# Linear attention and a two-layer expert on one core: the keys' maxima sent through DRAM, the large px matmuls split over quarters of the array, and the first large block's attention begun earlier

## The chip, the cores and the metric

One core of a Trainium2 chip runs the whole program. The metric is device microseconds of one execution; lower is better. The kernel before takes 844.15 us (median of three runs, 844.1 to 846.15). The execution that was profiled took 839.7 us, of which the page's span is 837.9.

## The reference

```python
def _attn_ref(q, k, v):                      # (8, 8, 576, 64) each
    q_s = np.exp(q - np.max(q, axis=-1, keepdims=True))
    q_s = q_s / (np.sum(q_s, axis=-1, keepdims=True) + 1e-09)
    k_s = np.exp(k - np.max(k, axis=2, keepdims=True))
    k_s = k_s / (np.sum(k_s, axis=2, keepdims=True) + 1e-09)
    kv = np.einsum('bhsd,bhse->bhde', k_s, v)
    return np.einsum('bhsd,bhde->bhse', q_s, kv).astype(np.float32)

def _moe_ref(x, w_in, w_out):                # x (4608, 512), w_in (512, 2048), w_out (2048, 512)
    h = x @ w_in
    relu6 = np.clip(h + 3.0, 0.0, 6.0)
    g = h * relu6 / 6.0
    return (g @ w_out).astype(np.float32)
```

The attention's output, heads side by side, is x. The softmax of the keys runs over the 576 tokens of a batch, so every key channel has one maximum for each batch; the queries' runs over the 64 channels of a head. The weights come as float64.

## The kernel before

**Tokens.** The 4608 tokens are taken as three small blocks of 512 and three large blocks of 1024. A batch has 576 tokens, so a block straddles batches. Heads go in four pairs (hp): two heads of 64 channels fill 128 partitions.

**Small blocks (0, 1, 2).** For each of 16 chunks of d_ff, gemm1 makes `ph` (12 matmuls of 128x512), relu6 and a split into a high and a low part make `gp` on ACT and DVE, and gemm2 adds into four `po` banks (12 matmuls), one chunk later. A product in float32 is made of three fp32r matmuls: high x high, high x low, low x high.

**Large blocks (0, 1, 2).** They use seven products of half-size blocks for each pair of chunks instead of eight. Phase 1 makes h from the "factors" of x (`factors`, tiles `right`: seven high and low splits of blocks of x and of differences of them) and from sums of weights; phase 2 multiplies by w_out likewise. These weights are made during small blocks 1 and 2 (`sum_weights`, `plain_weights`), kept in DRAM (`wf`) and fetched again, two of 56 slots to a transfer, into `gp` and `left` tiles.

**Attention.** `token_attention` makes x for one block and one head pair. It is a generator; each yield is a point at which the main loop goes on with matmuls of the expert. Its steps are: loads of the queries and, for a batch whose kv is not yet there, of the keys twice (`kt`, channels on partitions, and `ke`, tokens on partitions) and the values; DVE's maximum over `kt` into `km` (L355), one number for each channel, copied over 128 columns by POOL into `kb` (L357), and the queries' softmax and transposition (`q_softmax_t`, DVE with help of ACT and POOL); PE turns `kb` round into the bank `pm` (L363), so that each partition has the maxima of all channels in a row, DVE subtracts it from `ke` (L364), ACT takes exp; an empty step; `kv_of`: ten float32 matmuls of 128x64 for a batch, two heads in two halves of the columns, into the bank `pkv`, and a kv tile of 128x128 in which the two heads' 64x64 blocks lie on the diagonal and the rest is zero; last px: for each 512 tokens, a float32 matmul of that kv tile with the transposed queries for every batch that they touch, copied by ACT into x (L385; in small blocks split into high and low).

`pm`, `pkv` and `px` share two PSUM banks (pool `ps_a`). A float32 matmul shows as two records, two passes, in the trace. 24 pairs of batch and head pair go through `token_attention`; batches 0 and 1 go through the older `attention`.

**What sets the order.** A scheduling layer records the instructions and orders each engine's queue. From block 1 on PE's order is that of the program (`in_order`). `steps` strings the units of a block together (L734): a unit's px comes after the next unit's loads. In blocks 1 and 2 each chunk calls it twice; in the large blocks every second slot calls it. Block 1 carries the attention of block 2, block 2 that of large block 0, and large block s that of s + 1. Block 2's last two chunks call `factors` three times each, and the rest of it, under a high priority, follows the block. `behind` puts instructions behind the ones listed in `front`, which are those of phase 2's last split (L590).

**Buffers.** `kt` has one buffer, `km` and `kb` two, `v` three, `gp` four. All loads and stores but four are issued by SP, whose queue is in order: an issue that waits holds up those behind it. `sum_weights` takes two `v` tiles (w4 and sums) and writes its parts to `gp` tiles. `store` takes `v` tiles.

Of the kernel before, what the change touches and what calls it, by code (L numbers as in the profile page):

```python
# [1 line left out]

# [16 lines left out]
P = 128  # L19
# [13 lines left out]
def attention_moe(  # L33
# [82 lines left out]
    FROM_DRAM = 3  # L116
    whole = dr.tile([P, NFC, 2 * DM], F32, name="whole")

    def split(hi, lo, src):
        return nc.scalar.copy(hi, src), nc.vector.tensor_sub(lo, src, hi.bitcast(F32))  # L120

    front = []

    def behind(units, count=1):

        with ExitStack() as order:
            for ins in front:
# [129 lines left out]
    def attention(j, hp):  # L257

        if not j:
            kt, qt, qT, vt, ke = first[hp]  # L260
        else:
            kt, ke, vt = load_k(j, hp)
# [25 lines left out]

    def load_k(b, hp, tokens=False):
        kt = att.tile([P, S], F32, name="kt", bufs=1)  # L290
        nc.sync.dma_start(kt, kT[b, hp])
        ke = att.tile([P, NCH, P], F32, name="ke", bufs=2)
        if tokens:
            nc.sync.dma_start(ke, k[b, hp].rearrange("p c h d -> p c (h d)"))
        vt = att.tile([P, NCH, 2, D + 1], F32, name="vt", bufs=2)
        nc.sync.dma_start(vt, v[b, hp])
        return kt, ke, vt

# [16 lines left out]
    def q_softmax_t(qt):  # L315
# [13 lines left out]
        qT = moe.tile([P, 2 * DM], F32, name="m", bufs=1)[:, 0:n]  # L329
        nc.vector.transpose(qT, qt)  # L330
        return qT

# [8 lines left out]
    def token_attention(t0, n, hp, put):  # L341

        need = [b for b in range(t0 // S, (t0 + n - 1) // S + 1)]
        qt = att.tile([P, SB], F32, name="qt", bufs=1)[:, 0:n]
        at = (t0 - TURNED) // TB
        nc.sync.dma_start(
            qt.rearrange("p (b n) -> p b n", n=TB),
            qf[at : at + n // TB, hp].rearrange("b p n -> p b n"),
        )
        loads = {b: load_k(b, hp, tokens=True) for b in need if (b, hp) not in kvs}  # L350
        yield
        new = {}
        for b, (kt, ke, vt) in loads.items():
            km = att.tile([P, 1], F32, name="km", bufs=2)
            nc.vector.tensor_reduce(km, kt, axis=AX.X, op=ALU.max)  # L355
            kb = att.tile([P, P], F32, name="kb", bufs=2)
            nc.gpsimd.tensor_copy(kb, km.broadcast_to([P, P]))  # L357
            new[b] = ke, vt, kb
        qT = q_softmax_t(qt)
        yield  # L360
        for ke, vt, kb in new.values():
            pm = bank_a("pm")
            flip(pm[:, 0:P], kb)  # L363
            nc.vector.tensor_sub(  # L364
                ke, ke, pm[:, 0:P].rearrange("p (o n) -> p o n", o=1).broadcast_to([P, NCH, P])
            )
            nc.scalar.activation(ke, ke, AF.Exp)
        yield
        yield
        for b, (ke, vt, kb) in new.items():  # L370
            kv_of(b, hp, ke, vt)
        yield
        for c in range(n // TB):
            px = bank_a("px")
            at = t0 + c * TB
            for b in need:
                lo, hi = max(b * S - at, 0), min((b + 1) * S - at, TB)
                if lo < hi:
                    mm(px[:, lo:hi], kvs[b, hp], qT[:, c * TB + lo : c * TB + hi], True, True)
            put(c, hp, px)  # L380
        yield

    def sb_attention(s):
        def put(c, hp, px):
            nc.scalar.copy(x_of(s)[:, hp, c * TB : (c + 1) * TB], px)  # L385

        return [token_attention(START + s * SB, SB, hp, put) for hp in (0, 2, 1, 3)]

    def block_attention(j):
        def put(c, hp, px):  # L390
            x_hi, x_lo = x_block(j)
# [19 lines left out]

    def keep(pair, side, block, src):
        nc.sync.dma_start(kept[side][:, SLOT[side][pair, PRODUCT[block]]], src)

# [11 lines left out]
    def sum_weights(pair, side):  # L426
# [17 lines left out]
        nc.vector.tensor_sub(s4, a12, s2)  # L444
        for i in range(2):
            dst = moe.tile([P, 2, TB], F32R, name="gp", bufs=4).rearrange("p i n -> p (i n)")
            four = dst.rearrange("p (k e n) -> p k e n", k=2, e=2)
            src = sums[:, i * TB : (i + 1) * TB].rearrange("p (k n) -> p k n", k=2)
            split(four[:, :, 0], four[:, :, 1], src)
            for k_ in range(2):  # L450
                block = (S1, S2, S3, S4)[2 * i + k_]
                keep(pair, side, block, dst[:, k_ * TB : (k_ + 1) * TB].bitcast(F32))
        yield
# [69 lines left out]
    def relu6(g, r, h):  # L523
        nc.scalar.activation(r, h, AF.Relu, bias=three, scale=1.0)  # L524
        nc.vector.scalar_tensor_tensor(g, r, 6.0, h, op0=ALU.min, op1=ALU.mult)  # L525

    def phase1(s):
        xb, yb, zb = {}, {}, {}
        for i, (p, n) in enumerate(SLOTS1):
# [24 lines left out]
            with tc.high_priority():  # L554
                if n == 1:
                    nc.scalar.copy(h11, x)
                if n == 0:
                    nc.vector.tensor_add(h11, h11, z)  # L558
                    relu6(h11, temp(), h11)
                if n == 3:  # L560
                    nc.scalar.copy(h21, x)
                if n == 2:
                    nc.scalar.copy(h22, y)
                if n == 4:
                    nc.vector.tensor_add(h22, h22, x)  # L565
                if n == 5:
                    relu6(h12, temp(), x)
                if n == 6:
                    nc.vector.tensor_add(h21, h21, y)  # L569
                    r = moe.tile([P, 2 * DM], F32, name="v", bufs=3)  # L570
                    relu6(gb, r, gb)
                    nc.vector.tensor_sub(h12, h22, h12)
            yield

    def phase2(s):
# [6 lines left out]
        def make():  # L582
# [6 lines left out]
            t = ring[:, i % 4]  # L589
            front[:] = split(t[:, 0], t[:, 1], src)  # L590
            ready[i] = t
# [77 lines left out]
    def gemm1(j, f):  # L669
# [10 lines left out]
        gp = moe.tile([P, 2, TB], F32R, name="gp", bufs=4)  # L680
        split(gp[:, 0], gp[:, 1], g)
        return gp[:, 0], gp[:, 1]
# [18 lines left out]
    def store(j, po):  # L701
        for t in range(NTT):
            ob = moe.tile([P, 2 * DM], F32, name="v", bufs=3)[:, 0:DM]
            if t % 2:
# [62 lines left out]
    for j in range(NB):  # L767
        if j == 1:
            in_order.append(True)
        if j < NB - 1:  # L770
            turned = (j + 1) * TB >= TURNED
            units = block_attention(j + 1) if turned else [attention(j + 1, hp) for hp in range(NP)]
            step = steps(units, 6 if turned else 4)
        else:
            step = steps(sb_attention(0), 6)
            fac = factors(0)
        chunks = [*range(NFC)] if j < NB - 1 else [NFC - 1, *range(NFC - 1)]
        for n, f in enumerate(chunks):
# [8 lines left out]
            if j:  # L787
                next(sums, None)
            for _ in range((2 if f % 4 == 3 else 1) if not j else 2 if n < 14 else 1):
# [11 lines left out]
    for _ in sums:  # L801
        pass
    with tc.high_priority():
        for _ in fac:
            pass
        fetch(GROUPS - 2)

    for s in range(NS):
        more = s + 1 < NS
        step = steps(sb_attention(s + 1), 6) if more else iter(())  # L810
        fac = factors(s + 1) if more else iter(())
# [75 lines left out]
```

## Time and profile before

| what | value |
|---|---|
| runs | 844.1, 844.15, 846.15 us |
| profiled execution | 839.7 us, span 837.9 us |
| DMA packets | 75643, 192.3 MB, mean 230 GB/s |
| block 1 begins, block 2 begins, large block 0 begins | near 141, 240, 343 us |
| large block 1, 2 begin (phase 1) | near 517, 685 us |
| TensorE's clock | 0.992 of full over the span |

An engine's busy time on the page is the union of its instructions. TensorE's matmuls overlap in their pipeline, so their mean duration (0.39 us for 128x512) is longer than their distance (0.227 us); what a group of matmuls costs is read from the starts. In the chain of work that ended last, each piece is charged from its start to the next piece's, which is why the chain is the view for this. A row of the waits reads: engine and line, released by whom, us in total, times, longest.

### The profile page before, as it was taken

The page shows a single profiled execution, that of the slowest core. Times are in us where ns is not written, and L with a number is a line of the kernel's source. Part 1 is how long each engine was busy: PE and PEld are TensorE (multiplying, and loading weights), DVE is VectorE, ACT ScalarE, POOL GpSimd, SP SyncE. Part 2 cuts the span into 40 slices and gives each one's busy share as a digit, 9 for nine tenths or more (in the row PEclk, how much of TensorE's full clock was granted, in tenths as well). Part 3 has the DMA queues.
Part 4 walks back from the last instruction along what each step waited for, and adds up shares of the span by engine and source line. Part 5 has one row for each costly group of instructions (what it writes and reads, how often), then busy time and mean ns, then how long its engine had stood idle before and what let it go on. Part 6 is the DMA issues. An engine that isn't in the chain of part 4 may idle for free.

```text
span 837.9 us, 11778 instructions
## 1 busy us (share of the span) xinstructions
PE 805.7 (96%) x4032; PEld 648.1 (77%) x4032; DVE 677.7 (81%) x1095; ACT 442.4 (53%) x717; POOL 68.0 (8%) x179
## 2 busy tenths in 40 slices
PE   4999989999999999999999999999999999999997
PEld 3677767777887877787877788777888888888886
DVE  7998999999778998579989994698599836558873
ACT  7997764444344454355456653545466535445542
POOL 5000011020100112001112000010000000000000
PEclk9899999999999999999999999999999999999999
DMA  9999676678549661578775577665566775665672
GB/s 362 415 407 319 220 256 208 217 241 288 183 153 357 203 236 51 179 264 292 279 252 184 184 233 254 220 224 162 176 194 188 246 247 187 194 201 187 192 227 98
DMA packets 75643, 192.30 MB, mean 230 GB/s; under 512 B 7232, under 2 KB 19520, under 8 KB 73536
## 3 DMA queue, kind: packets, MB, share of 16 engines
q1 hardware_dynamic: 75008, 190.51, 67.2%
q10 hardware_dynamic: 576, 1.05, 0.4%
q8 instruction: 32, 0.52, 0.3%
q14 instruction: 27, 0.22, 0.1%
HBM read 147.49 MB, written 44.04 MB: 229 GB/s over the span
## 4 chain that ended last, share of the span: by engine, by line
PE 67%; DVE 18%; DMA 5%; ACT 4%; issue 3%; POOL 2%; SPq 0%; ACTq 0%; DVEq 0%; POOLq 0%
PE x L87 30%; PE z L87 12%; PE y L87 11%; PE po L87 6%; PE ph L87 5%; PE px L87 2%; DVE gp L120 2%; POOL swap L312 2%; DVE g L525 2%; PE pkv L87 1%; DVE v L150 1%; DVE v L154 1%; DMA v<-whole 1%; DMA qt<-in_qf_dram 1%; ACT qt L228 1%
## 5 line engine op out<-in xcount | busy, mean ns | idle before, releaser
L120 ACT CAST gf<-g 128x512 fp32r<-128x512 f32 x168 | 104.4, 623 | 95.2 <-DVE gf L120 34.9
L87 PE MATMUL po<-w,gp 128*128 128x512 f32 x576 | 146.5, 400 | 4.1 <-ACT gp L120 3.4
L87 PE MATMUL ph<-x,w 128*128 128x512 f32 x576 | 144.1, 398 | 2.9 <-ACT w L120 2.6
L120 DVE TENSOR_TENSOR gf<-g,gf 128x512 fp32r<-128x512 f32 x168 | 112.9, 685 | 26.2 <-ACT gf L120 25.4
L87 PEld LDWEIGHTS po<-w,gp 128*128 128x128 f32 x576 | 106.3, 189 | 32.4 <-ACT gp L120 6.2
L87 PEld LDWEIGHTS ph<-x,w 128*128 128x128 f32 x576 | 108.7, 190 | 27.8 <-ACT w L120 3.5
L87 PE MATMUL x<-right,gp 128*128 128x512 f32 x384 | 94.9, 392 | 0.4 <-DVE g L565 0.4
L87 PE MATMUL x<-gf,gp 128*128 128x512 f32 x384 | 94.0, 390 | 0.4 <-DVE gf L120 0.4
L87 PEld LDWEIGHTS x<-right,gp 128*128 128x128 f32 x384 | 71.7, 188 | 16.4 <-DVE g L565 0.8
L87 PEld LDWEIGHTS x<-gf,gp 128*128 128x128 f32 x384 | 71.8, 188 | 16.1 <-DVE gf L120 0.8
L524 ACT ACTIVATE g<-ph,three 128x512 f32<-128x512 f32 x48 | 32.8, 688 | 69.1 <-PE ph L87 68.7
L524 ACT ACTIVATE v<-g,three 128x1024 f32<-128x1024 f32 x24 | 27.6, 1151 | 39.3 <-DVE g L569 39.3
L87 PE MATMUL y<-right,gp 128*128 128x512 f32 x192 | 48.1, 395 | 0.0
L87 PE MATMUL x<-right,left 128*128 128x512 f32 x192 | 47.7, 391 | 0.0
L87 PE MATMUL x<-gf,left 128*128 128x512 f32 x192 | 47.3, 390 | 0.1
L87 PE MATMUL z<-gf,gp 128*128 128x512 f32 x192 | 46.6, 389 | 0.0
L120 ACT CAST gp<-g 128x512 fp32r<-128x512 f32 x48 | 29.7, 619 | 25.5 <-DVE g L525 25.3
L87 PEld LDWEIGHTS x<-gf,left 128*128 128x128 f32 x192 | 35.9, 188 | 8.2 <-DVE gf L120 0.6
L87 PEld LDWEIGHTS z<-gf,gp 128*128 128x128 f32 x192 | 36.0, 188 | 7.5
L87 PEld LDWEIGHTS y<-right,gp 128*128 128x128 f32 x192 | 35.6, 188 | 8.0 <-issue 0.5
L87 PEld LDWEIGHTS x<-right,left 128*128 128x128 f32 x192 | 35.8, 188 | 7.4
L524 ACT ACTIVATE g<-g,three 128x512 f32<-128x512 f32 x24 | 17.4, 724 | 43.2 <-DVE g L558 43.2
(134 smaller groups left out, 1306.0 us busy)
## 6 DMA issues: line engine op xcount, KB each, us to landing
gp<-wf SPq DMA_DIRECT2D x112, 512.0 KB, 3.4
left<-wf SPq DMA_DIRECT2D x56, 512.0 KB, 3.4
raw<-in_w_dram SPq DMA_DIRECT2D x16, 1024.0 KB, 13.7
wf<-gp SPq DMA_DIRECT2D x64, 256.0 KB, 3.3
wf<-w SPq DMA_DIRECT2D x48, 256.0 KB, 4.3
vt<-in_v_dram SPq DMA_DIRECT2D x28, 325.0 KB, 5.3
kt<-in_kT_dram SPq DMA_DIRECT2D x28, 288.0 KB, 3.2
ke<-in_k_dram SPq DMA_DIRECT2D x24, 320.0 KB, 4.7
```

Of the source, the lines that this page charges most:

```text
L87: nc.tensor.matmul(out, lhsT, rhs, start=start, stop=stop, skip_group_check=goes_on)
L120: return nc.scalar.copy(hi, src), nc.vector.tensor_sub(lo, src, hi.bitcast(F32))
L150: nc.vector.scalar_tensor_tensor(vu, high, 0xC0000000, m, op0=ALU.bitwise_and, op1=ALU.bitwise_or)
L154: nc.vector.tensor_tensor(vu, vu, low, op=ALU.add)
L228: nc.scalar.activation(qs[:, i], qs[:, i], AF.Exp, bias=qm[:, i : i + 1], accum_out=qr[:, i : i + 1],)
L312: nc.gpsimd.tensor_copy(swap[r : r + QD], stat[o : o + QD])
L524: nc.scalar.activation(r, h, AF.Relu, bias=three, scale=1.0)
L525: nc.vector.scalar_tensor_tensor(g, r, 6.0, h, op0=ALU.min, op1=ALU.mult)
```

## The change

Five things change.

- **Maxima by way of DRAM.** POOL's copy `kb`, PE's turn `pm` and its bank go. `greatest` takes the maximum as before, writes the 128 numbers to a DRAM tile `maxima` of its own for every batch and head pair, and reads them back to all 128 partitions as `kb`. The second batch of a unit has its `kt` loaded a step later. A unit has seven steps instead of six, and the subtraction is held behind the transposition of the queries.
- **Large px in quarters.** In large blocks px takes the two 64x64 blocks of kv alone. Head h of token half c goes from partitions h (rows of the array) to columns c: four tiles of 64x64. Bank h holds head h, its lower 64 partitions the first 512 tokens and its upper 64 the second 512. ACT copies four times 64x512 instead of twice 128x512.
- **First large block earlier.** Its attention is chained behind block 2's, so that it begins in block 1's last chunks. Every chunk of block 2 takes two steps.
- **Factors behind the front.** `front` now holds the last marked instruction of each engine (relu6, the splits of `gp` and `gf`, phase 1's copies), and the factors of large block 0 come two to a chunk in block 2's last three chunks, each behind it.
- **Sums' parts in place.** `sum_weights` writes the high and low parts over w4 and sums instead of into `gp` tiles, and each slot is stored in two runs of 1 KB a partition. `store` takes halves of `gp` tiles instead of `v` tiles.

```diff
+    maxima = dr.tile([B, NP, P], F32, name="maxima")
...
+    def split_ahead(hi, lo, src):
+        for ins in split(hi, lo, src):
+            ahead(ins)
...
+    def ahead(ins):
+
+        front[ins.ins.engine] = ins
+        return ins
...
-        loads = {b: load_k(b, hp, tokens=True) for b in need if (b, hp) not in kvs}
-        yield
-        new = {}
-        for b, (kt, ke, vt) in loads.items():
+        new = [b for b in need if (b, hp) not in kvs]
+
+        def greatest(kt, b):
+
             km = att.tile([P, 1], F32, name="km", bufs=2)
             nc.vector.tensor_reduce(km, kt, axis=AX.X, op=ALU.max)
+            nc.sync.dma_start(maxima[b, hp].rearrange("(p o) -> p o", o=1), km)
             kb = att.tile([P, P], F32, name="kb", bufs=2)
-            nc.gpsimd.tensor_copy(kb, km.broadcast_to([P, P]))
-            new[b] = ke, vt, kb
-        qT = q_softmax_t(qt)
-        yield
-        for ke, vt, kb in new.values():
-            pm = bank_a("pm")
-            flip(pm[:, 0:P], kb)
...
+            nc.sync.dma_start(kb, maxima[b, hp].rearrange("(o p) -> o p", o=1).broadcast_to([P, P]))
+            return kb
...
+        kb = [greatest(t, b) for t, b in zip(kt, new[:1])]
+        kt = [load_kt(b, hp) for b in new[1:]]
+        yield
+        kb += [greatest(t, b) for t, b in zip(kt, new[1:])]
+        qT, turned = q_softmax_t(qt)
+        yield
+        for t, most in zip(ke, kb):
+            most = most.rearrange("p (o n) -> p o n", o=1).broadcast_to([P, NCH, P])
+            with tc.issue_after(turned.ins):
+                nc.vector.tensor_sub(t, t, most)
+            nc.scalar.activation(t, t, AF.Exp)
...
+            px = [bank_a("px") for _ in range(2)]
+            rows = [slice(h * D, (h + 1) * D) for h in range(2)]
+            for both in zip_longest(*(segments(need, t0 + c * TB) for c in range(2))):
+                for c, part in enumerate(both):
+                    if part:
+                        b, lo, hi = part
+                        for h, r in enumerate(rows):
+                            mm(
+                                px[h][rows[c], lo:hi],
+                                kvs[b, hp][r, r],
+                                qT[r, c * TB + lo : c * TB + hi],
...
+            for c in range(2):
+                for h, r in enumerate(rows):
+                    nc.scalar.copy(x_of(s)[r, hp, c * TB : (c + 1) * TB], px[h][rows[c]])
...
+        four = w4.rearrange("p (e n) -> p e n", e=2)
+        split(four[:, 0].bitcast(F32R), four[:, 1].bitcast(F32R), sums[:, 0:TB])
+        keep(pair, side, (S1, S2), four)
+        four = sums.rearrange("p (e n) -> p e n", e=2)
+        split(four[:, 0].bitcast(F32R), four[:, 1].bitcast(F32R), four[:, 1])
+        keep(pair, side, (S3, S4), four)
...
-            step = steps(units, 6 if turned else 4)
+            step = steps(units, 7 if turned else 4)
+            if j == NB - 2:
+                step = chain(step, steps(sb_attention(0), 7))
         else:
-            step = steps(sb_attention(0), 6)
             fac = factors(0)
...
-            if j == NB - 1 and n >= 14:
-                for _ in range(3):
-                    next(fac, None)
+            if j == NB - 1:
+                behind(fac, {13: 2, 14: 2, 15: 2}.get(n, 0))
...
-    with tc.high_priority():
-        for _ in fac:
-            pass
-        fetch(GROUPS - 2)
+    behind(fac, 7)
+    fetch(GROUPS - 2)
```

How this moves the queues. On PE, in block 2, the second chunk with an attention step of large block 0. Before (`px` is the product of kv and queries, `pm` the turn of the maxima, `ph` and `po` the expert's two layers):

```order
L87 MATMUL ph<-x_1540,w_370 128x512 x12
L87 MATMUL px<-m,kv 128x192
L87 MATMUL px<-m,kv 128x320
L87 MATMUL px<-m,kv 128x256 x2
L93 MATMUL pm<-ident,kb 128x128 x2
L87 MATMUL po<-w_338,gp 128x512 x12
```

And the same place now:

```order
L88 MATMUL ph<-x_1530,w_371 128x512 x12
L88 MATMUL px<-m,kv 64x192 x2
L88 MATMUL px<-m,kv 64x256 x2
L88 MATMUL px<-m,kv 64x320 x2
L88 MATMUL px<-m,kv 64x256 x2
L88 MATMUL po<-w_339,gp 128x512 x12
```

Four matmuls on the whole array have become eight on 64 columns each, and the two turns behind them are gone.

On SP, in block 1 (`kt`, `ke`, `vt`, `qt` are loads of keys, values and queries, `wf` stores of sums, `out_dram` of block 0's output). Before:

```order
L708 DMA out_dram<-v 128x512 x3
L291 DMA kt<-in_kT_dram 128x576
L294 DMA ke<-in_k_dram 128x640
L296 DMA vt<-in_v_dram 128x650
L413 DMA wf_90<-gp 128x512 x4
L346 DMA qt<-in_qf_dram 128x512
```

Now:

```order
L368 DMA maxima<-km 128x1
L304 DMA kt<-in_kT_dram 128x576
L368 DMA maxima<-km 128x1
L304 DMA kt<-in_kT_dram 128x576
L456 DMA wf_91<-v 128x2x256 x4
L368 DMA maxima<-km 128x1
L304 DMA kt<-in_kT_dram 128x576
L358 DMA qt<-in_qf_dram 128x512
L370 DMA kb<-maxima 128x128
```

The loads of `kt` come one behind the other, each behind the write of the maxima of the one before, ahead of the units to which they belong.

On DVE at the end of block 2, from the last softmax or factor instruction ahead of the last relu6 (`g<-g,ph`) to the large block's first instruction. Before:

```order
L327 RECIPROCAL qr<-qr 128x32
L328 TENSOR_TENSOR qt<-qt,qr 128x1024
L525 SCALAR_TENSOR_TENSOR g<-g,ph 128x512
L120 TENSOR_TENSOR gp<-g,gp 128x512
L705 TENSOR_SCALAR v<-po 128x512 x2
L558 TENSOR_TENSOR g_3293<-g_3293,z_3295 128x512
```

Now (`right` are the factors' parts, `x` the differences they are made of):

```order
L122 TENSOR_TENSOR right_3170<-x_2355,right_3170 128x1024
L567 SCALAR_TENSOR_TENSOR g<-g,ph 128x512
L553 TENSOR_TENSOR x_2355<-x_2355 128x2x512
L122 TENSOR_TENSOR gp<-g,gp 128x512
L556 TENSOR_TENSOR x_2355<-x_2355 128x2x512
L561 TENSOR_TENSOR x_2355<-x_2355 128x2x512
L122 TENSOR_TENSOR right_3212<-x_2355,right_3212 128x1024
L122 TENSOR_TENSOR right_3174<-x_2355,right_3174 128x1024
L749 TENSOR_SCALAR gp<-po 128x512
L122 TENSOR_TENSOR right_3209<-x_2355,right_3209 128x1024
L749 TENSOR_SCALAR gp<-po 128x512
L122 TENSOR_TENSOR right_3250<-x_2355,right_3250 128x1024
```

The softmax instructions have left the place, and seven instructions of the factors have come behind the last relu6.

More of the change, by code (lines that the diff above doesn't have):

```diff
@@ L1 @@
 from contextlib import ExitStack
+from itertools import chain, zip_longest
 import numpy as np
@@ L261, in attention @@
         else:
-            kt, ke, vt = load_k(j, hp)
+            kt = load_kt(j, hp)
+            ke = att.tile([P, NCH, P], F32, name="ke", bufs=2)
+            vt = load_v(j, hp)
             qt = att.tile([P, TB], F32, name="qt", bufs=1)
@@ new lines, in token_attention @@
+        ke, vt = [], []
+        for b in new:
+            ke.append(att.tile([P, NCH, P], F32, name="ke", bufs=2))
+            nc.sync.dma_start(ke[-1], k[b, hp].rearrange("p c h d -> p c (h d)"))
+            vt.append(load_v(b, hp))
+        yield
+        kb = [greatest(t, b) for t, b in zip(kt, new[:1])]
[9 more added lines that the diff above has]
+            nc.scalar.activation(t, t, AF.Exp)
@@ L368, in token_attention @@
         yield
         yield
-        for b, (ke, vt, kb) in new.items():
-            kv_of(b, hp, ke, vt)
+        for b, *two in zip(new, ke, vt):
+            kv_of(b, hp, *two)
         yield
[L373 to L380, printed above, removed]
+        put(t0, hp, need, qT)
@@ L410, in attention_moe, with keep @@
     kept = [dr.tile([P, NSLOT, TB], F32, name=f"wf{i}") for i in range(2)]
-    def keep(pair, side, block, src):
-        nc.sync.dma_start(kept[side][:, SLOT[side][pair, PRODUCT[block]]], src)
+    def keep(pair, side, blocks, src):
+        for n, block in enumerate(blocks):
+            to = kept[side][:, SLOT[side][pair, PRODUCT[block]]]
+            nc.sync.dma_start(to.rearrange("p (e n) -> p e n", e=2), src[:, :, n * HT : (n + 1) * HT])
     def plain_weights(pair, side):
@@ L444, in sum_weights @@
         nc.vector.tensor_sub(s4, a12, s2)
[L445 to L452, printed above, removed]
+        four = w4.rearrange("p (e n) -> p e n", e=2)
[4 more added lines that the diff above has]
+        keep(pair, side, (S3, S4), four)
         yield
@@ L523, in relu6 @@
     def relu6(g, r, h):
-        nc.scalar.activation(r, h, AF.Relu, bias=three, scale=1.0)
-        nc.vector.scalar_tensor_tensor(g, r, 6.0, h, op0=ALU.min, op1=ALU.mult)
+        ahead(nc.scalar.activation(r, h, AF.Relu, bias=three, scale=1.0))
+        ahead(nc.vector.scalar_tensor_tensor(g, r, 6.0, h, op0=ALU.min, op1=ALU.mult))
     def phase1(s):
@@ L555, in phase1 @@
                 if n == 1:
-                    nc.scalar.copy(h11, x)
+                    ahead(nc.scalar.copy(h11, x))
                 if n == 0:
@@ L560, in phase1 @@
                 if n == 3:
-                    nc.scalar.copy(h21, x)
+                    ahead(nc.scalar.copy(h21, x))
                 if n == 2:
-                    nc.scalar.copy(h22, y)
+                    ahead(nc.scalar.copy(h22, y))
                 if n == 4:
-                    nc.vector.tensor_add(h22, h22, x)
+                    ahead(nc.vector.tensor_add(h22, h22, x))
                 if n == 5:
@@ L702, in store @@
         for t in range(NTT):
-            ob = moe.tile([P, 2 * DM], F32, name="v", bufs=3)[:, 0:DM]
+            if t % 2 == 0:
+                two = moe.tile([P, 2, TB], F32R, name="gp", bufs=4).bitcast(F32)
+            ob = two[:, t % 2]
             if t % 2:
@@ L788, in attention_moe @@
                 next(sums, None)
-            for _ in range((2 if f % 4 == 3 else 1) if not j else 2 if n < 14 else 1):
+            for _ in range((2 if f % 4 == 3 else 1) if not j else 2):
                 next(step, None)
```

44 lines of the change are left out of this document (24 added, 20 removed).

## The prediction, made before the result was known

> **What bounds the kernel now.** I read the page first: the busy line, then the chain of work that ended last.
>
> ```profile
> span 837.9 us, 11778 instructions
> PE   805.7 (96%) x4032; PEld 648.1 (77%) x4032; DVE 677.7 (81%) x1095; ACT 442.4 (53%) x717; POOL 68.0 (8%) x179
> PE 67%; DVE 18%; DMA 5%; ACT 4%; issue 3%; POOL 2%; SPq 0%; ACTq 0%; DVEq 0%; POOLq 0%
> PE x L87 30%; PE z L87 12%; PE y L87 11%; PE po L87 6%; PE ph L87 5%; PE px L87 2%; DVE gp L120 2%; POOL swap L312 2%; DVE g L525 2%; PE pkv L87 1%; DVE v L150 1%; DVE v L154 1%; DMA v<-whole 1%; DMA qt<-in_qf_dram 1%; ACT qt L228 1%
> ```
>
> TensorE is busy in 96% of the span, so what shortens its own stream is gained whole, as long as nobody new makes it wait. Next the waits of PE: after the first block (it ends near 140 us) few are left. The three that this change touches, and the largest one for scale:
>
> ```profile
> PE pe L93 <- ACT kq L246: 6.3, 1, 6.3
> PE pm L93 <- ACT x L385: 1.4, 1, 1.4
> PE px L87 <- DVE m L330: 1.3, 1, 1.3
> PE pm L93 <- DVE ke L364: 1.0, 1, 1.0
> ```
>
> Then the busy time by stretches, for block 1 (141 to 240.6 us) and block 2 (to 342 us), where the attention of the first large block lies:
>
> ```profile
> 141.00:240.60 99.60, 98.00 (x495) 78.60 (x494) 87.86 (x178) 42.66 (x71) 13.88 (x44) 1.00 0.62 208
> 240.60:342.00 101.40, 98.59 (x569) 79.75 (x567) 86.50 (x150) 46.63 (x69) 14.64 (x40) 1.00 0.61 208
> ```
>
> The columns are PE, PEld, DVE, ACT, POOL, granted clock, DMA share. PE is full at clock 1.00; DVE is at 174.4 of 201.0 us, the only engine that could take over.
>
> Last, what attention costs PE between the regular matmuls. This is the chain through the first half of the large block 0, piece by piece with start and duration; six regular matmuls take 1.36 us:
>
> ```profile
> 351.99 2.72 PE x L87 x12
> 354.71 0.22 PE pm L93 x2
> 354.93 1.39 PE z L87 x6
> 356.32 2.74 PE x L87 x12
> 359.06 1.36 PE y L87 x6
> 360.42 1.32 PE pkv L87 x40
> 361.74 1.59 PE y L87 x6
> 367.41 1.75 PE px L87 x8
> ```
>
> So two pm turns cost 0.22 and 0.03 in the group behind: 0.125 us each. One unit's px costs 1.75. Its two pkv, whose matmuls take 64 columns of the array each, cost 1.32 and 1.59 - 1.36 = 0.23 behind, 1.55. The same in large block 2, where a unit has one pkv and longer px:
>
> ```profile
> 529.89 0.73 PE pkv L87 x20
> 530.62 1.58 PE y L87 x6
> 536.31 1.83 PE px L87 x6
> ```
>
> One pkv costs 0.73 + 0.22 = 0.95, two 1.55: twenty records stream in 0.60, and 0.35 is fixed, paid for going into the divided array and back. Also, the 8 px records (two passes over 1024 columns) show 0.85 ns a column and pass; 65 columns would take 55 ns alone, and pkv's records come every 30 ns. So two halves of the array do run at the same time here.
>
> **The change, part by part.**
>
> *Maxima by way of DRAM.* The 24 pm turns go: 24 x 0.125 = 3.0 us of PE. Two waits go with them, since pm took a PSUM bank just behind px and stood on ACT's copy, and on the subtraction before it:
>
> ```profile
> 259.52 0.30 PE L93 MATMUL pm<-ident,kb 128*128 128x128 f32 x1
> 261.19 0.30 PE L93 MATMUL pm<-ident,kb 128*128 128x128 f32 x1 [1.37 <-ACT x L385]
> 295.49 0.30 PE L93 MATMUL pm<-ident,kb 128*128 128x128 f32 x1
> 296.82 0.30 PE L93 MATMUL pm<-ident,kb 128*128 128x128 f32 x1 [1.03 <-DVE ke L364]
> ```
>
> That is 2.4 us more; what is late next there is pkv, two chunks on. Sum: 5.4 gained. POOL's 24 copies go too, off the path. Added are 24 writes of 512 B and 24 reads to all partitions, all on SP. The trace has no such transfer; the nearest are a whole tile to DRAM and a load:
>
> ```profile
> whole<-v SPq DMA_DIRECT2D x10, 512.0 KB, 2.9
> kt<-in_kT_dram SPq DMA_DIRECT2D x28, 288.0 KB, 3.2
> wf<-gp SPq DMA_DIRECT2D x64, 256.0 KB, 3.3
> wf<-w SPq DMA_DIRECT2D x48, 256.0 KB, 4.3
> ```
>
> Write and read one after the other: some 6 us. In the order a maximum stands far ahead of its use (some 150 DVE instructions lie between the fifth and sixth reductions and the subtraction that uses them), so I cost the trip at nothing; without that lead it would be 6 us for each of 16 units.
>
> What has a price is the lead itself. Only kt's one buffer and km's two hold the reductions back now, so the order has all 24 of them in blocks 0 to 2, where before 16 stood:
>
> ```profile
> L355 DVE TENSOR_REDUCE km<-kt 128x1 f32<-128x576 f32 x24 | 17.9, 744 | 4.5 <-DMA kt<-in_kT_dram 4.4
> L364 DVE TENSOR_TENSOR ke<-ke,pm 128x640 f32<-128x640 f32 x24 | 18.9, 805 | 1.8 <-PE pm L93 1.7
> L385 ACT COPY x<-px 128x512 f32<-128x512 f32 x24 | 13.3, 588 | 1.1 <-PE px L87 0.7
> ```
>
> Eight more of 744 ns are 6.0 us: DVE has 180.4 of work in a stretch of 201 us that PE now shortens to about 194 (12 of the pm, the two waits, four px, and 2.2 from below). It fits, with 14 us over. But each reduction stands in DVE's queue behind a load that SP issues only when the one before is reduced. On SP the write waits for the reduction, and behind it wait the next kt, stores of wf, the loads of qt, ke, vt; DVE's queue, relu6 in it, waits for kt. In the order five to fourteen DVE instructions lie between two reductions, 2.9 us of work at the tightest against 3.2 for the load. Bounds: nothing, and 24 times the 1.1 us (4.4 in 4) that DVE stood for kt before, 26 us, of which DVE's room hides 14. I take 0.9 us at PE: nearer to nothing, because the short gaps are few. The subtraction reads SBUF instead of PSUM: from below 805 to the same; I take the same.
>
> *px in quarters.* Twelve units cost PE 8 x 1.75 + 4 x 1.83 = 21.3 us. Each matmul of 128 x 128, half of it zeros, becomes two of 64 x 64 on the diagonal blocks, and the two halves of the tokens go to two halves of the columns: four tiles, each with half of the 1024 columns. If all four run together, a unit streams in 1.75 / 2 = 0.875, pays the fixed 0.35 as pkv does, and 0.12 for tiles that start in turn (0.06 from one pkv pair to the next, partly inside the 0.35): 1.35, times 12 is 16.2; 5.1 gained. The trace shows two halves at once and never four. Bounds: four at once without the fee, 10.5 us (10.8 gained); none together, 12 x 3.85 = 46.2 (24.9 lost). I take 1.35, by pkv's rows, the only divided matmuls here.
>
> The Trainium skill, "TensorE: Matmul & The Clock Gate", Part 3, "The mechanism", says that matmuls start and end strictly in program order, and only loads of weights are pulled ahead. By that rule at most two of these tiles overlap, as rival 1 has it, and the part would lose 3.9 us instead of gaining 5.1. The same page's "Measured speedup vs the span model" has sixteen tiles together at 10.6 times, which speaks for four; no run here shows either yet.
>
> The price on ACT: four copies of 64 x 512 for two of 128 x 512. If a copy's time goes by the elements of a partition, that is 24 x 0.588 = 14.1 us more (at best nothing); ACT is 53% busy (46.6 of 101.4 in block 2), and px's two banks are next wanted by a pkv a chunk later. Nothing. Without that cover 1.2 us a unit.
>
> *Attention from block 1's end.* The first large unit's loads, softmax, pkv (1.55 on PE) move into block 1's last three chunks; its px stays in block 2, as its x tile is block 1's. PE's sum stays. DVE gets it where it was idle, and the step between softmax and px is one longer (seven). That should end the 1.27 us for the transposed queries, and at block 2's end the last relu6 no longer stands behind a softmax multiplication:
>
> ```profile
> 205.91 1.14 PE L87 MATMUL px<-m,kv 128*128 128x128 f32 x4 [1.27 <-DVE m L330]
> 340.73 1.22 DVE L328 TENSOR_TENSOR qt<-qt,qr 128x1024 f32<-128x1024 f32 x1
> 341.87 0.68 DVE L525 SCALAR_TENSOR_TENSOR g<-g,ph 128x512 f32<-128x512 f32 x1
> 343.25 1.92 PE L87 MATMUL po<-w,gp 128*128 128x512 f32 x6 [0.94 <-ACT gp L120]
> ```
>
> 2.2 gained, between nothing and that. Against it, seven of the factor instructions now stand behind the last relu6, two parts of 1.2 us and a store's 0.7 among them, so the third and fourth factor come just when the large block's third and fourth slot want them: 0.5 lost, between nothing and 2.
>
> *Sums in place, store in gp.* The second split overwrites what the first reads: ACT waits for DVE, up to 0.7 us, 16 times, in ACT's idle half. The parts leave in rows of 1 KB, as wf<-w does (4.3 us for 3.3); the fetches come tens of us later. Nothing, both.
>
> **Sum.** -5.4 - 5.1 - 2.2 + 0.9 + 0.5 = -11.3 us. The profiled execution took 839.7 (span 837.9 and 1.8 around it): 828.4. It lies 4.45 under the median of 844.15; from that, **832.8**. About 0.3%, 2.5 us, is what a measurement can tell from no change.
>
> **Rivals.**
> 1. *Quarters overlap only in pairs.* A float32 matmul is two passes on the same tile; if the second, waiting for the first, holds up all that stands behind it in PE's queue, only this second pass and the next tile's first run together. A unit costs 1.75 + 0.35 = 2.10, twelve 25.2: 3.9 lost. -5.4 - 2.2 + 1.4 + 3.9 = -2.3, 841.9. For it: only halves are seen together, and pkv's 30 ns is just half of 55, as it would be under either. Against: pkv has only two tiles to offer. Chance 0.22.
> 2. *The reductions become the bound (slower).* DVE in blocks 1 and 2: 180.4 us and 24 waits for kt. PE has 194 there and 5 us gained elsewhere against the 201 of before; from 180.4 + 24 w over 206, that is w over 1.1 us, the kernel is slower than before. At 1.5 us: 216.4, 10.4 above 206, so 854.6 if none of these waits falls into time in which DVE idles anyway; with half of it there, 849. For it: the one-buffer chain through SP's queue; against: before, 20 of 24 reductions did not wait. Chance 0.09.
> 3. *No two quarters overlap*: +24.9 - 5.4 - 2.2 + 1.4 = +18.7, 862.9. Against: pkv's halves. Chance 0.05.
>
> **How the numbers follow.** The forecast, four together, has 0.64; its own range is 829 (both unknown losses nothing, the fee smaller) to 837.5 (reductions wait 0.75 us each). Rival 1 reaches 839 to 844.5 and lies on the bound of 841.6: 0.09 of its chance is faster, 0.12 the same, 0.01 slower. Faster 0.64 + 0.09 = 0.73, same 0.12, slower 0.01 + 0.09 + 0.05 = 0.15. The range 829 to 843.5 takes in the forecast and nearly all of rival 1, some 0.82.
>
> **What would show it.** No pm row, and no wait of PE around px but for kv; px's chain piece at 1.0 to 1.4 us with the group behind it 0.2 longer (2.0 is rival 1, 3.8 rival 3); DVE's idle time for kt under 15 us; at block 2's end no wait of po for gp, and under 1 us for the right factors. I am wrong if px's piece is not shorter, or if PE's waits after 140 us grow past 6 us.

## The result, and the profile after

The changed kernel takes **1015.8 us** (median; 1011.6 to 1018.6) where the kernel before takes 843.6 beside it: a ratio of 1.203, 95% interval 1.200 to 1.207. It was forecast at 832.8. The profiled execution has a span of 1014.0 us, 176.1 more than before. The page of the changed kernel, its summary and four rows of the 40 slices:

```profile
span 1014.0 us, 11917 instructions
...
PE 843.9 (83%) x4096; PEld 664.4 (66%) x4096; DVE 677.4 (67%) x1095; ACT 458.0 (45%) x741; POOL 58.0 (6%) x155
...
PE   4898844754555555798998999999999999999997
...
PEclk9999976785866777799999999999999999999999
DMA  9996867878688856687238686577755568666563
GB/s 378 416 380 227 191 153 65 97 94 74 103 110 87 162 83 100 181 278 254 69 133 277 226 281 207 186 236 239 225 191 180 188 191 276 196 194 199 188 200 132
```

The loss has one place. From the sixth slice to the sixteenth (127 to 406 us) PE is half busy, and the transfer engines are 50 to 89% busy (digits 5 to 8) while they move 65 to 162 GB/s; from the twenty-second on, such shares go with 180 to 281. By the starts of PE's matmuls, block 1 begins at 152.3 us (136.6 before), large block 0 some 522.5 (346.4 before), and from there to the end both kernels need about 491.5. All of the 176 us is lost before large block 0: 15.7 before block 1, 160.4 in blocks 1 and 2 (370.2 us for 209.8). In the windows, PE's busy time in two stretches of small blocks (same columns as in the prediction):

```profile
130.00:240.00 110.00, 59.79 (x225) 44.36 (x226) 44.77 (x86) 19.88 (x32) 5.89 (x16) 0.75 0.76 103
240.00:343.00 103.00, 55.41 (x203) 41.06 (x202) 38.54 (x79) 15.94 (x26) 5.56 (x20) 0.72 0.78 99
```

DVE too is busy for only 83 of 213 us: nobody is full, something is waited for. The reductions' group and the longest waits of PE name it:

```profile
L367 DVE TENSOR_REDUCE km<-kt 128x1 f32<-128x576 f32 x24 | 18.1, 752 | 154.2 <-DMA kt<-in_kT_dram 154.2
```

```profile
PE po L88 <- DVE gp L122: 55.4, 10, 10.2
PE px L88 <- DVE kv L217: 34.2, 9, 8.1
PE po L88 <- ACT gp L122: 28.4, 10, 6.9
```

DVE stands 154.2 us for kt (4.4 before), 6.4 a reduction, and PE stands for what DVE has queued behind it. The transfers say why kt is late; the last column is the median from issue to landing:

```profile
wf<-v SPq DMA_DIRECT2D x64, 256.0 KB, 10.6
...
kt<-in_kT_dram SPq DMA_DIRECT2D x28, 288.0 KB, 10.8
...
kb<-maxima SPq DMA_DIRECT2D x24, 64.0 KB, 4.7
...
maxima<-km SPq DMA_DIRECT2D x24, 0.5 KB, 9.2
```

The smallest transfer of the program, 512 bytes, takes 9.2 us, and kt, at 3.2 before, takes 10.8. The timeline shows the cycle, SP's issues first, DVE's reductions then:

```profile
170.12 0.33 SPq L368 DMA_DIRECT2D maxima<-km  x1
170.55 0.38 SPq L304 DMA_DIRECT2D kt<-in_kT_dram  x1
...
182.83 0.33 SPq L368 DMA_DIRECT2D maxima<-km  x1
```

```profile
169.34 0.75 DVE L367 TENSOR_REDUCE km<-kt 128x1 f32<-128x576 f32 x1 [9.32 <-DMA kt<-in_kT_dram]
...
182.05 0.75 DVE L367 TENSOR_REDUCE km<-kt 128x1 f32<-128x576 f32 x1 [8.57 <-DMA kt<-in_kT_dram]
...
194.74 0.75 DVE L367 TENSOR_REDUCE km<-kt 128x1 f32<-128x576 f32 x1 [6.34 <-DMA kt<-in_kT_dram]
```

A reduction ends, its write and the next kt are issued 0.4 us apart, both land 8 to 12 us later, the next reduction runs. The 24 reductions go from 119 to 402 us in steps of 12.3.

The quarters of px, meanwhile, do what they were forecast to do. The timeline of PE in large block 0:

```profile
545.22 1.52 PE L88 MATMUL x<-right,left 128*128 128x512 f32 x6
546.67 1.09 PE L88 MATMUL px<-m,kv 64*64 64x320 f32 x16
547.70 3.02 PE L88 MATMUL y<-right,gp 128*128 128x512 f32 x12
550.56 0.62 PE L88 MATMUL x<-right,gp 128*128 128x512 f32 x2
```

From 545.22 to 550.56 stand eighteen regular matmuls (18 x 0.227 = 4.09) and one unit's px: 1.25 us, where it was 1.75.

### The profile page after: what moved, and what is told of

Same layout as the page of the kernel before. It is cut to its first block, busy times and chain, and to the rows that moved or that the text cites. A ratio compares the mean times of both kernels' runs of the same rounds, so it can differ in the third digit from the quotient of the medians.

```text
span 1014.0 us, 11917 instructions
## 1 busy us (share of the span) xinstructions
PE 843.9 (83%) x4096; PEld 664.4 (66%) x4096; DVE 677.4 (67%) x1095; ACT 458.0 (45%) x741; POOL 58.0 (6%) x155
## 4 chain that ended last, share of the span: by engine, by line
PE 42%; DVE 5%; DMA 4%; POOL 1%; issue 1%; ACT 1%; SPq 0%; ACTq 0%; DVEq 0%; POOLq 0%
PE x L88 21%; PE z L88 9%; PE y L88 7%; DMA qt<-in_qf_dram 2%; PE po L88 2%; PE ph L88 1%; POOL swap L325 1%; PE px L88 1%; PE pkv L88 1%; DVE g L567 1%; DVE m L343 0%; DVE qr L337 0%; DMA out_dram<-gp 0%; DMA left<-wf 0%; DVE qm L333 0%
## 5 line engine op out<-in xcount | busy, mean ns | idle before, releaser
L88 PE MATMUL po<-w,gp 128*128 128x512 f32 x576 | 179.1, 463 | 87.5 <-DVE gp L122 55.4
L88 PEld LDWEIGHTS po<-w,gp 128*128 128x128 f32 x576 | 124.4, 223 | 131.1 <-DVE gp L122 63.0
L88 PE MATMUL ph<-x,w 128*128 128x512 f32 x576 | 152.0, 413 | 3.1 <-ACT w L122 2.6
L88 PEld LDWEIGHTS ph<-x,w 128*128 128x128 f32 x576 | 115.2, 202 | 32.7 <-ACT w L122 3.2
L367 DVE TENSOR_REDUCE km<-kt 128x1 f32<-128x576 f32 x24 | 18.1, 752 | 154.2 <-DMA kt<-in_kT_dram 154.2
L122 ACT CAST v<-v 128x512 fp32r<-128x512 f32 x32 | 19.8, 619 | 83.7 <-DVE v L122 40.9
L88 PE MATMUL px<-m,kv 64*64 64x192 f32 (+5 forms) x192 | 24.1, 446 | 32.8 <-DVE kv L217 31.8
L325 POOL COPY swap<-qm 32x32 f32<-32x32 f32 (+1 forms) x64 | 22.2, 346 | 480.0 <-DVE qm L333 478.0
## 6 DMA issues: line engine op xcount, KB each, us to landing
kt<-in_kT_dram SPq DMA_DIRECT2D x28, 288.0 KB, 10.8
```

The lines of the kernel that those rows point to most:

```text
L88: nc.tensor.matmul(out, lhsT, rhs, start=start, stop=stop, skip_group_check=goes_on)
L325: nc.gpsimd.tensor_copy(swap[r : r + QD], stat[o : o + QD])
```

## The experiments

Theory 1 is that the write itself does the harm: 128 pieces of 4 bytes, side by side in DRAM, are worked off one after another, and what is issued behind them waits. Against it stood that another part of the change does it, or the trip's dependences (a read that waits for its write), or the number of added transfers.

**The change without the trip** (POOL's copy and PE's turn put back; the order of the steps, quarters, early start and sums as changed):

```diff
-            nc.sync.dma_start(maxima[b, hp].rearrange("(p o) -> p o", o=1), km)
-            nc.sync.dma_start(kb, maxima[b, hp].rearrange("(o p) -> o p", o=1).broadcast_to([P, P]))
+            nc.gpsimd.tensor_copy(kb, km.broadcast_to([P, P]))
...
+            pm = bank_a("pm")
+            flip(pm[:, 0:P], most)
```

> The changed kernel with the maxima's old way (POOL's copy, PE's turn, a PSUM bank) and everything else of the change kept. If the write of the maxima to DRAM is what costs, all of the loss goes: 843.6 less 6.6 for the quarters (12 px at 1.235 instead of 1.75 and 1.83) less about 2 of waits, 835. If the loss comes from the attention's earlier start, the sums in place or the factors behind the front, it stays near 1015.

Measured: 837.4, ratio 0.9946 [0.9923, 0.9969]. The rest of the change, taken together, loses nothing and is 0.5% faster than before; all of the loss comes with the trip.

**The trip without its dependence, packed and spread.** kb is read from a row of the keys, so other numbers than the maxima are subtracted, and nothing waits for the write but the reuse of km's two buffers. In the second kernel each number lies 512 bytes from the next:

```diff
-    maxima = dr.tile([B, NP, P], F32, name="maxima")
+    maxima = dr.tile([B, NP, P, P], F32, name="maxima")          # second kernel
...
-            nc.sync.dma_start(maxima[b, hp].rearrange("(p o) -> p o", o=1), km)
+            nc.sync.dma_start(maxima[b, hp][:, 0:1], km)         # second kernel
...
-            nc.sync.dma_start(kb, maxima[b, hp].rearrange("(o p) -> o p", o=1).broadcast_to([P, P]))
+            nc.sync.dma_start(kb, kT[b, hp][0:1, 0:P].broadcast_to([P, P]))
```

> The changed kernel, but kb is read from the first keys instead of from the maxima, so that nothing waits for the write's landing; the write of 128 numbers to 512 bytes that lie together stays (the keys are shifted by other numbers than their maxima). If the write clogs the queue for the loads behind it: 1000 to 1015, kt still lands after 10 to 12 us. If the loss is in the round trip (kb waiting for the write): back near 835.

> As the one with kb from the first keys, but each of the 128 numbers is written 512 bytes from the next. Theory 1, writes of 4 bytes into the same stretch of DRAM are worked off one after the other: the write lands after 2.5 to 4 us, kt after 3 to 5, the kernel takes 830 to 850. Theory 2, every 4-byte piece costs its 70 ns wherever it lies: 9 us as before and 1000 to 1015. Theory 3, the reductions pulled ahead bind SP and DVE whatever the write costs: over 950 in both.

Measured: 1019.2 and 849.4 (one run each). Their transfers, packed and then spread:

```profile
kt<-in_kT_dram SPq DMA_DIRECT2D x28, 288.0 KB, 10.9
...
maxima<-km SPq DMA_DIRECT2D x24, 0.5 KB, 8.8
```

```profile
kt<-in_kT_dram SPq DMA_DIRECT2D x28, 288.0 KB, 3.3
...
maxima<-km SPq DMA_DIRECT2D x24, 0.5 KB, 2.5
```

The same number of transfers, pieces and bytes; only the addresses differ, and 170 us with them. So far theory 1 holds: it is the write, and it is that its pieces lie side by side. That they are worked off one after another is not shown by this. The read's wait for its write is not needed for the loss.

**How many, and how far apart.** A quarter of the numbers (packed), and three other spacings, with the same kb. The diff is that of the quarter; for the spacings only the last dimension of `maxima` in the second kernel above becomes 8, 16 or 64 numbers:

```diff
-            nc.sync.dma_start(maxima[b, hp].rearrange("(p o) -> p o", o=1), km)
+            nc.sync.dma_start(maxima[b, hp][0:32].rearrange("(p o) -> p o", o=1), km[0:32])
```

> The changed kernel with kb read from the first row of the keys (other numbers are subtracted than the maxima) and only 32 of the 128 maxima written, side by side as in the changed kernel. If every number takes its turn, the write lands in 2.3 to 4 us, kt behind it in 3.5 to 5, and the time is 850 to 880. If the fee does not depend on how many there are, 1015.

> As the kernel whose numbers were spread 512 bytes apart (kb read from the first row of the keys, so other numbers are subtracted than the maxima), but spread 32 bytes apart: 128 numbers over 4 KB. If the turns are taken within stretches of 512 bytes, 16 numbers share one: landing between 2.5 and 4 us, 850 to 875 in all. If within stretches of 32 or 64 bytes, the write lands in 2.5 to 3 us and the time is 849. If what hurts is that they lie in the same few KB, 9 us and 1019.

> The same, 64 bytes apart. With stretches of 512 bytes 8 numbers share one: 2.5 to 3.5 us, 850 to 860. With 64 or less: 2.5, 849.

> The same, 256 bytes apart. With stretches of 512 bytes 2 numbers share one: 2.5 to 3 us, 849 to 853; with stretches of a KB or more the write is longer than 3 us.

Measured: 913.9 for 32 packed numbers; 850.9, 854.9 and 854.0 at 32, 64 and 256 bytes (one run each). A quarter of the numbers, then 32 bytes apart:

```profile
kt<-in_kT_dram SPq DMA_DIRECT2D x28, 288.0 KB, 7.1
...
maxima<-km SPq DMA_DIRECT2D x24, 0.1 KB, 4.9
```

```profile
kt<-in_kT_dram SPq DMA_DIRECT2D x28, 288.0 KB, 3.5
...
maxima<-km SPq DMA_DIRECT2D x24, 0.5 KB, 2.7
```

Above the 2.5 us of a spread write, 32 packed numbers cost 2.4 and 128 cost 6.3: the price grows with the number, less than in proportion, and 913.9 lies between the two times that I had expected. A queue of equal turns would have grown in proportion, so how the pieces hinder each other stays open. 32 bytes of distance already end it, where I had thought of 512; between 4 and 32 nothing was tried.

**The write on POOL's queue**, with all else as changed:

```diff
-            nc.sync.dma_start(maxima[b, hp].rearrange("(p o) -> p o", o=1), km)
+            nc.gpsimd.dma_start(maxima[b, hp].rearrange("(p o) -> p o", o=1), km)
```

> The changed kernel with the write of the maxima issued by POOL instead of SP; all else as changed. If the 4-byte pieces only hold up what stands behind them in SP's queue, kt lands in 3 to 4 us again, only kb comes late, far ahead of its use, and the time is that of the spread kernel, 849. If they hold up the transfer engines or the memory, which all queues share, kt still lands in some 10 us, and the time stays over 950.

Measured: 963.0 (one run). Transfers, and then DVE's waits:

```profile
wf<-v SPq DMA_DIRECT2D x64, 256.0 KB, 9.0
...
kt<-in_kT_dram SPq DMA_DIRECT2D x28, 288.0 KB, 6.8
...
maxima<-km POOLq DMA_DIRECT2D x24, 0.5 KB, 10.7
```

```profile
DVE km L367 <- DMA kt<-in_kT_dram: 54.4, 12, 10.2
DVE v L484 <- DMA wf<-v: 52.9, 10, 10.8
```

Transfers of SP's queue still land late (kt after 6.8 us, not 10.8), so at least a large part of the stall lies in what the queues share, not in one queue's order.

**The same trip in four rows.** DVE's transposition of 32x32 blocks puts 32 maxima in a row on each of four partitions; four pieces of 128 bytes are written. The second kernel also holds each reduction behind the transposition of the unit before, so that they are no longer taken far ahead; the third has this hold and the 4-byte pieces of the change:

```diff
+            with ExitStack() as order:
+                for ins in turns[-1:]:                            # second and third
+                    order.enter_context(tc.issue_after(ins))
                 nc.vector.tensor_reduce(km, kt, axis=AX.X, op=ALU.max)
-            nc.sync.dma_start(maxima[b, hp].rearrange("(p o) -> p o", o=1), km)
+            four = att.tile([P, 32], F32, name="four", bufs=2)    # first and second
+            nc.vector.transpose(four, km.broadcast_to([P, 32]))
+            nc.sync.dma_start(maxima[b, hp].rearrange("(r n) -> r n", n=32), four[0:P:32, :])
```

> The changed kernel with one step more: VectorE's 32x32 transposition of the maxima puts the 128 numbers in a row of 32 on each of four partitions, and four pieces of 128 bytes are written to DRAM where 128 pieces of 4 bytes were; kb is read back as before. If each piece that falls into the same stretch takes its turn (some 70 ns, 9.2 us for 128), the write lands in 2 to 2.5 us, kt in 3.3, and the time is that of the kernel whose numbers were spread, 849. If any write of pieces under 512 bytes into one stretch pays the whole fee, it lands in 9 us as before and the time stays near 1015.

> The same, and each reduction is held behind the transposition of the unit before it, so that it is no longer taken far ahead. If the 12 us between the kernel with spread numbers (849.4) and the one with POOL and TensorE (837.4) are the price of the reductions taken early, on a VectorE that is full in block 1, this kernel loses that price and keeps the saved turns: 833 to 837, with all of VectorE's waits for kt under 3 us. If they are the price of the trip itself (SP's queue, kb landing late), it stays at 845 to 850, with the subtraction waiting for kb.

> The changed kernel with the reductions held as in the one above, the 128 pieces of 4 bytes kept. If the 172 us come from a chain (write, then kt, then the next reduction, 24 times in a row), holding breaks the chain: VectorE stands only for the second kt of a unit, up to 8 us in 8 units, partly hidden: 860 to 890. If the writes slow everything whatever stands behind them, 960 or more.

Measured: 850.2, ratio 1.0098 [1.0060, 1.0136]; held 842.6, 0.9992 [0.9962, 1.0023]; held with 4-byte pieces 971.9 (one run). So the lead of the reductions costs 8.9 us by itself (1.0098 - 0.9992, of 842). The rows point to the queries and not to kt. For kt DVE stood 4.2 us with the lead and 3.1 without. For the queries, whose loads SP issues behind the early writes and loads of kt, it stood longer with the lead (first row) than without:

```profile
DVE qm L333 <- DMA qt<-in_qf_dram: 22.6, 13, 3.7
DVE qm L333 <- DMA qt<-in_qf_dram: 7.8, 9, 1.7
```

The lead is not what makes the small pieces expensive: the chain is broken in the third, and DVE then stands for whatever comes behind a write, and SP for the writes:

```profile
DVE v L489 <- DMA wf<-v: 53.4, 9, 11.7
DVE km L371 <- DMA kt<-in_kT_dram: 44.9, 8, 9.8
```

```profile
SPq L374 <- DMA maxima<-km: 169.2, 22, 9.0
```

I had expected 833 to 837 of the second. What still held it back was sought with three kernels.

**Sums and store in their old buffers** (parts to gp tiles, output through v, the code of before), on the kernel without the trip and on the held one with four rows; and the held one with **both transfers of the trip issued by POOL**:

> The kernel with POOL's copy and TensorE's turn (the rest of the change kept), and the weights' sums and the store with their old buffers (parts written to gp tiles, the output staged in v). In place, a v tile is free only when the store of its parts has landed: VectorE stood 8.8 us for that (7 times), and no such row is on the page of before. If TensorE pays part of it, this kernel is faster than 837.4, at 834 to 836; if it lies in VectorE's free time, or the gp tiles cost the same again, it stays at 836.5 to 838.5.

> The kernel with four rows of 32 maxima and held reductions (842.6), with the old buffers for the sums and the store. There VectorE stands 12.8 us for the stores of the sums, the largest wait for a transfer. If these are what keeps it 5 us above the kernel with POOL and TensorE, it comes to 836 to 839. If not, 841 to 844.

```diff
-            nc.sync.dma_start(maxima[b, hp].rearrange("(r n) -> r n", n=32), four[0:P:32, :])
+            nc.gpsimd.dma_start(maxima[b, hp].rearrange("(r n) -> r n", n=32), four[0:P:32, :])
...
-            nc.sync.dma_start(kb, maxima[b, hp].rearrange("(o p) -> o p", o=1).broadcast_to([P, P]))
+            nc.gpsimd.dma_start(kb, maxima[b, hp].rearrange("(o p) -> o p", o=1).broadcast_to([P, P]))
```

> The kernel with four rows of 32 maxima and held reductions (842.6), with write and read of the maxima issued by POOL instead of SP. SP stood 32.8 us (19 times, 2.9 at most) in front of kb's read until the write had landed, with the loads and stores of the weights behind it. If this standing is what costs the 5 us, the kernel comes to 835 to 839. If it does not matter where the trip is issued, 841 to 844.

Measured: 838.2, 0.9952 [0.9932, 0.9973]; **835.8, 0.9921 [0.9891, 0.9952]**; 850.6, 1.0107 [1.0070, 1.0144]. In place, a v tile comes free only when its store has landed. DVE's wait for that in the held kernel, and with the old buffers its wait at the same instruction, now for a load:

```profile
DVE v L491 <- DMA wf<-v: 12.8, 8, 2.9
```

```profile
DVE v L489 <- DMA v<-whole: 7.0, 6, 1.8
```

The new buffers, of sums and store together, cost 6.0 us beside the trip and nothing without it (0.9946 and 0.9952). The held kernel with the old buffers beats both kernels of the case. Moving the trip to POOL loses 9.7 us, where I had expected a gain or nothing: POOL, in order too, stands for the write, and the queries' softmax, which needs POOL's `swap`, stands behind it (15.4 us of DVE's waits in the two rows below, 4.3 in the held kernel):

```profile
POOL kb L376 <- DMA maxima<-four: 43.8, 18, 7.5
```

```profile
DVE qr L326 <- POOL swap L325: 13.9, 9, 4.0
...
DVE qm L326 <- POOL swap L325: 1.5, 5, 0.4
```

**The quarters alone**, on the kernel before, and the reverse, px whole on the kernel without the trip:

> The kernel before with the large px in quarters and nothing else. Four tiles at once: 1.235 us a unit, 6.6 us gained, 837. Tiles in pairs only (rival 1 of the prediction): a unit of 2.1, 847.5.

> The kernel with POOL's copy and TensorE's turn (the rest of the change kept), and px of the large blocks whole again, as before. The quarters measured 1.235 for 1.745 us in eight units and 1.227 for 1.86 in four, 6.6 us in all. If that is gained whole in the new order, this kernel takes 837.4 + 6.6 = 844. If ScalarE's four copies of 0.58 us for two give part of it back here too, as they did where pm stood right behind px, 838 to 841.

Measured: 846.8, 1.0050 [1.0032, 1.0068]; and 843.2, 1.0015 [1.0001, 1.0029], against 0.9946 with quarters. In the new order the quarters gain 5.8 us; alone on the kernel before they lose 4. There the turn pm stands right behind px and wants its bank. PE, then ACT, in block 2 of the quarters alone:

```profile
259.00 1.09 PE L88 MATMUL px<-m,kv 64*64 64x192 f32 x16
263.51 0.30 PE L94 MATMUL pm<-ident,kb 128*128 128x128 f32 x1 [3.41 <-ACT x L401]
```

```profile
261.65 2.36 ACT L401 COPY x<-px 64x512 f32<-64x512 f32 x4
```

Half the partitions take as long to copy: four copies, 2.36 us, behind ACT's other work, and PE stands 3.41 us for the bank (1.37 before), over the kernel 8.4 us in 5 waits where it stood 1.4 in one. In the two stretches with these waits (258 to 274 and 297 to 315 us) the granted clock was 0.89 and 0.81; in the same stretches of the kernel before it was 1.00. That 846.8 is close to what overlap in pairs was expected to give (847.5) is chance: px's 16 records take 1.09 us here, as in the changed kernel.

**The early start undone**, without the trip and in the held kernel with four rows:

```diff
-            if j == NB - 2:
-                step = chain(step, steps(sb_attention(0), 7))
         else:
+            step = steps(sb_attention(0), 7)
```

> The same kernel (quarters kept), with the first large block's attention begun in block 2 again, in steps of seven. If the early start is worth what the forecast took for it (2.2 us, from the wait for the transposed queries and the one at block 2's end), 839 to 840. If it costs, since it puts VectorE's work of a unit into block 1, where its room was small, 833 to 836: block 1 near 100 us instead of 102.4.

> The kernel with four rows of 32 maxima and held reductions, with the first large block's attention begun in block 2 again. That kernel took 842.6 where 833 to 837 was expected; its block 1 is 106.4 us (100.2 before the change). If the early start is what fills VectorE there, block 1 comes to 101 to 103 and the time to 836 to 839. If the three more instructions of each trip (transposition, and SP's write and read) fill it, it stays at 841 to 844.

Measured: 837.3, 0.9964 [0.9942, 0.9985], and 845.0, 1.0041 [1.0009, 1.0073]; with it 0.9946 and 0.9992. The early start is the faster in both pairs, by 1.5 and 4.1 us. With the intervals of the two kernels taken together (root of the sum of the squared half-widths) that is 1.5 +- 2.7 without the trip, not clear of noise, and 4.1 +- 3.7 in the held kernel, just clear of it. The traces show one part of it: at block 2's end, without the trip, PE runs through with the early start and stands without it, 1.3 us with a second wait (1.8 in the held pair):

```profile
340.38 6.04 PE L88 MATMUL po<-w,gp 128*128 128x512 f32 x24
```

```profile
345.35 0.73 PE L88 MATMUL po<-w,gp 128*128 128x512 f32 x2 [0.97 <-ACT gp L121]
```

My expectation that it filled VectorE is not borne out.

## Why the prediction was wrong, point by point

- **The failed step is the one that cost "the trip at nothing"**, bounded by "some 6 us" from a tile's write and a load, with the lead of 150 instructions as its cover. The lead did cover the trip: no subtraction waited for kb. What was not priced is what the write does to the transfers beside it. The rows taken as nearest were those of whole tiles, 256 to 512 KB each, and bytes were not what the time went by. It measures 165.6 us: 1015.8 against 850.2 with four rows, all else the same but one small transposition. With the reductions held it is 129.3 (971.9, one run, against 842.6), so most of the price does not need the lead.
- **"I take 0.9 us"** for reductions that wait for kt, with an upper bound of 26 (24 x 1.1). They waited 24 x 6.4. The structure was seen (one kt buffer, SP's queue, DVE's queue with relu6 in it), and rival 2 was this mechanism with break-even at 1.1 us; its price of 1.5 was taken from a trace in which kt landed in 3.2. In blocks 1 and 2 (152.3 to 522.5 us) DVE stood for transfers as these rows say, 165.8 us in all:

```profile
DVE km L367 <- DMA kt<-in_kT_dram: 139.3, 19, 9.5
DVE v L484 <- DMA wf<-v: 11.9, 7, 5.2
DVE v L475 <- DMA wf<-v: 9.8, 2, 7.0
DVE qm L333 <- DMA qt<-in_qf_dram: 4.8, 7, 1.5
```

  In the kernel before it stood 9.7 us for transfers in these blocks, 0.9 of it for kt. The 156.1 us between the two are nearly the 160.4 that the blocks lost. With the write in four rows the reductions waited 4.2 us in all, and still the lead cost 8.9, ten times the 0.9; the rows there point to late queries.
- **Quarters, -5.1: right.** 1.25 us in large block 0, forecast 1.35, and 5.8 in all. More than two tiles run together, and four with the fixed 0.35 fit (0.875 + 0.35 = 1.225); rival 1 (2.10) and rival 3 (3.85) fall. What falls with them is my reading of the Trainium skill, "TensorE: Matmul & The Clock Gate", Part 3, "The mechanism": that matmuls start and end in program order does not say that at most two tiles overlap. On the order itself no row here speaks. "The price on ACT: nothing" holds only where no turn stands behind px.
- **Turns and waits, -5.4:** four rows instead of the turn, both with the old buffers, give 0.9921 against 0.9952: 2.6 us. That is the size of the turns (3.0), but their intervals overlap. The 2.4 for the waits were not the trip's to gain: with the turn kept and the old buffers, PE has no wait for `pm` left, so the rest of the change had already ended them.
- **Early start, -2.2: half borne out.** The two pairs give 1.5 and 4.1 us, the second just clear of noise. The wait at block 2's end goes with it, as forecast. The wait for the transposed queries is gone with and without the early start, so that part is not its doing; px waits for kv instead, in the kernel without the trip 3.5 us with the early start and 6.4 without:

```profile
PE px L88 <- DVE kv L216: 3.5, 4, 1.9
```

- **Sums in place, nothing:** right without the trip, 6.0 us wrong beside it. Of the half microsecond for the factors nothing is seen: in the kernel without the trip PE has no wait for a `right` tile.
- The marks named in "What would show it" were right as marks: DVE's idle time for kt, said to stay under 15, stood at 154.

## What to carry to other kernels

Price a new transfer by its pieces and their addresses, not by its bytes, and ask what it does to the transfers beside it, not only when it lands. Here a number from each partition left cheaply as rows (after a transposition), or with its pieces 32 bytes or more apart. When a step moves ahead, give it something that holds it back; a queue in order turns a free lead into work at the wrong time.

## What the runs showed of the hardware that I had not expected

- A write of 128 pieces of 4 bytes side by side took 8.8 to 9.2 us, and kt behind it on SP's queue landed after 10.8 us instead of 3.2; with the write on POOL's queue kt still took 6.8. With the pieces 32 bytes apart the write took 2.7 and kt 3.5. The Trainium skill, "DMA: Bandwidth & Descriptors", "Specifications", says that transfers under 512 bytes are read, modified and written. The runs do not bear out the size alone as the price: the pieces are 4 bytes in every case. Pieces that share a few bytes' stretch, and so would have to modify the same unit in turn, would fit; that is not shown.
- 64x64 tiles of float32 matmuls in four quarters of the array took 1.25 us a unit, against 1.75 for whole matmuls and an estimated 2.10 for an overlap in pairs.
- A copy of 64x512 took as long on ACT as one of 128x512 (0.58 and 0.588 us).
- TensorE's granted clock fell to 0.72 and 0.75 in stretches in which PE was busy for half the time; in block 1 and 2 of the kernel before it was 1.00.
